# Loading the inputs on one queue in the order of need, keeping TensorE busy until the first projection, and counting table loads in the schedule model

## The chip, the cores and the metric

The kernel runs on one core of a Trainium2 chip. The metric is the time of one execution in microseconds on the device; lower is better. The engines are TensorE (PE: matmuls and their weight loads), ScalarE (ACT), VectorE (DVE), GpSimd (POOL) and SyncE (SP, which issues nearly all transfers here). Each has its own instruction stream and runs it in order; semaphores tie the streams together.

## The reference

Two branches work on the same input x of 2048 tokens by 512 features, in bfloat16, and a gate for each token mixes them.

```python
x = A_x                                            # (1, 2048, 512)
g = sigmoid((x * gate_w).sum(-1, keepdims=True))
return g * A(x, wq, wk, wv, wo, beta) + (1 - g) * B(x, w_gate, w_up, w_down)
# B: (gelu(x @ w_gate) * (x @ w_up)) @ w_down, 1792 hidden features
# A: 32 heads of 16, 4 segments of 512 tokens; for each segment s:
logits = qs @ ks.T * scale + causal_mask;  a_dot = softmax(logits) @ vs
pq = phi(qs)                                       # phi(t) = t+1 if t > 0 else exp(t)
a_mem = (pq @ M) / (pq @ z + 1e-6)
o = sigmoid(beta) * a_mem + (1 - sigmoid(beta)) * a_dot
M = M + phi(ks).T @ vs;  z = z + phi(ks).sum()     # then the next segment; o @ wo at the end
```

So segment s+1 needs the memory M, z of segments up to s, but only its own K, Q and V for the softmax part.

## The kernel before, in words

All weights stay in SBUF. The work goes by segment: `prep(s)` projects K, Q and V from the transposed input `xT` (three buffers), `memory(s)` builds phi(K) and adds to M, z (`mzacc`, `mzbd`), `attention(s)` computes the logits into the four PSUM banks `psXALL` (L703), takes Exp on ScalarE (L711, 20 activations of 128x2048 a segment), masks on GpSimd (L723), multiplies with V into the one bank `psP` (L736), transposes and normalises on VectorE (`norm`, L756 to L764). `ups` and `downs` are the second half of branch B and the output products. All projections, gates, ups and downs share three PSUM banks `psW`; their matmuls all have line L408, their evictions L422 (ScalarE) or L425 (VectorE).

ScalarE must change its function table between Exp and Gelu. So the program has four phases: in phase p all Exp work of segment p (and the preparations of the next segment that need Exp), then a run of Gelu activations (`gelu_phase`: from SBUF at L802, from PSUM at L813), then Exp again. Each change shows as an ACT_TABLE_LOAD.

The order of instructions on every engine is made by a list scheduler, `Sched`, when the program is built. A task has an estimated duration for each engine it may run on, and a priority: the longest chain of estimates behind it plus a bias. At each step the scheduler takes the task with the earliest possible start, then the higher priority. Transfers are modelled with 330 KB per us behind one another. The durations of tasks decide the order alone; on the chip, semaphores decide when each instruction runs. In the model an Exp activation of 128x2048 is `act_t(2048)`, and the first Gelu of a phase has 1.3 added; the first Exp after a Gelu phase, named `exp{s}_0A0`, has nothing added.

At the start of the program:

- `warmP` and `warm0` to `warm7` (L491, L495) are nine matmuls on zeros, with nothing to wait for but a VectorE memset.
- x for segment 0 comes in four transfers of 128 KB into `hT[1]` (named `xin`), issued by SP. TensorE transposes it (`x0t0` to `x0t3`, L500, four 128x128 each against `ident`) into `psW` banks, and ScalarE and VectorE copy it to `xT[0]`.
- wk, wq and the vector gate_w are issued by ScalarE; wv, beta, the first half of w_gate (`wg`), the four transposing transfers of x for segment 1 (`xdma(1)`, L435), the second half of wg, w_up, w_down and wo by SP, in that order. SP's order comes from `rank`, which falls by 20 for each transfer and is its bias; the four small `betaT` transfers have no bias and come after wo.
- Later SP issues further transposing transfers: phi(K) into `phkt` for the memory, x for segments 2 and 3, and `otok` into `oT`; and the 16 output tiles.

The memory part of segment s (`prep` of s > 0) runs during phase s-1: `den` and four `num` products into `psW`, read by VectorE into `ndsc` and `otok` (L637 to L650).

Of the kernel before, what the change touches and what calls it, by code (L numbers as in the profile page):

```python
# [6 lines left out]
PE, ACT, DVE, POOL, SP = "pe", "act", "dve", "pool", "sp"  # L7
# [10 lines left out]
DF = 1792  # L18
NFT = 14
P = 128  # L20
# [293 lines left out]
def mm_t(n):  # L314
    return max(0.026, n / 2370.0)
# [14 lines left out]
def build(nc, A_x, A_wq, A_wk, A_wv, A_wo, A_beta, B_x, B_w_gate, B_w_up, B_w_down, gate_w, out):  # L330
    with ExitStack() as es:
        return _build(es, nc, A_x, A_wq, A_wk, A_wv, A_wo, A_beta, B_w_gate, B_w_up, B_w_down, gate_w, out)


def _build(es, nc, A_x, A_wq, A_wk, A_wv, A_wo, A_beta, B_w_gate, B_w_up, B_w_down, gate_w, out):
    def sb(name, shape, dtype=BF):
        return es.enter_context(nc.sbuf_tensor(name, shape, dtype))
# [15 lines left out]
    hT = [sb(f"hT{i}", [P, NFT, 512]) for i in range(2)]  # L353
# [6 lines left out]
    gatew = sb("gatew", [P, 4])  # L360
# [8 lines left out]
    betaT = sb("betaT", [P, 8])  # L369
# [8 lines left out]
    wq = sb("wq", [P, 4, 512])  # L378
    wk = sb("wk", [P, 4, 512])
    wv = sb("wv", [P, 4, 512])  # L380
    wo = sb("wo", [P, 4, 512])
    wg = sb("wg", [P, 4, DF])
# [5 lines left out]
    Pb = es.enter_context(nc.psum_tensor("psP", [P, 512], F32))  # L388
# [9 lines left out]
    def sem(name):  # L398
        nsem[0] += 1
        return es.enter_context(nc.semaphore(f"{name}_{nsem[0]}"))  # L400

    S = Sched(N_W)

    def task(name, eng, instrs, **kw):
        return S.add(Task(name, {eng: instrs}, **kw))
# [12 lines left out]
    def copy_out(name, g, dst, src, reads, writes, n, engs=(ACT, DVE), **kw):  # L418

        alts = {}  # L420
        if ACT in engs:
            alts[ACT] = [Instr(lambda e: e.activation(dst(), src(), ACTF.Copy), reads=reads, writes=writes,  # L422
                               est=act_t(n))]
        if DVE in engs:
            alts[DVE] = [Instr(lambda e: e.tensor_copy(dst(), src()), reads=reads, writes=writes,  # L425
                               est=dve_t(n))]
        return S.add(Task(name, alts, grp=g, **kw))

    def dma(name, eng, out_ap, in_ap, reads, writes, nbytes, issue=0.7, transpose=False, bias=0.0, sm=None,
            nonc=False):  # L430
        sm = sm if sm is not None else sem("d")

        def f(e):
            if transpose:
                return e.dma_start_transpose(out_ap(), in_ap())  # L435
            if nonc:
                with nc.allow_non_contiguous_dma(reason="small vector"):
                    return e.dma_start(out_ap(), in_ap())
            return e.dma_start(out_ap(), in_ap())
        return task(name, eng, [Instr(f, reads, writes, issue, dma_sem=sm)], bias=bias, nbytes=nbytes)  # L440

    rank = [9000.0]

    def wdma(key, eng, dst, src, nbytes, nonc=False):
        rank[0] -= 20.0
        dma("w_" + str(key), eng, lambda: dst, lambda: src, [], [("w", key)], nbytes, bias=rank[0], nonc=nonc)

    def xdma(s):
        for kb in range(4):
            rank[0] -= 20.0  # L450
            dma(f"x{s}_{kb}", SP, lambda kb=kb: xT[s % NX][:, kb, :],
                lambda kb=kb: A_x[0, s * 512:(s + 1) * 512, kb * 128:(kb + 1) * 128],
                [], [("xT", s % NX, kb)], 131072, issue=1.25, transpose=True, bias=rank[0] if s < 2 else 0.0)

    r4 = lambda w: w.rearrange("(kb p) n -> p kb n", p=P)
    wgr, wur = r4(B_w_gate), r4(B_w_up)
    half = 7 * 128

    warm = PT[R_PT - 1][:, 0, :]
    wkey = ("PT", R_PT - 1)  # L460
# [6 lines left out]
    task("tload", ACT, [Instr(lambda e: e.activation(stmp[:, 0:1], warm[:, 0:1], ACTF.Exp), reads=[wkey],  # L467
                              writes=[("stmp",)], est=1.5)], bias=8000.0)
    xin = hT[1][:, 0:4, :]
    for a in range(4):  # L470
        rank[0] -= 20.0
        dma(f"x0_{a}", SP, lambda a=a: xin[:, a, :], lambda a=a: A_x[0, a * 128:(a + 1) * 128, :], [],
            [("hT", 1, a)], 131072, bias=rank[0])
    wdma("wk", ACT, wk[:], r4(A_wk), 524288)
    wdma("wq", ACT, wq[:], r4(A_wq), 524288)
    wdma("gatew", ACT, gatew[:], gate_w.rearrange("(kb p) -> p kb", p=P), 1024, nonc=True)
    wdma("wv", SP, wv[:], r4(A_wv), 524288)
    wdma("beta", SP, betab[:], A_beta.partition_broadcast(P), 8192)
    for g in range(4):
        bsrc = A_beta.rearrange("(t g j) -> g t j", g=4, j=2)[g]  # L480
        dma(f"betaT{g}", SP, lambda g=g: betaT[32 * g:32 * g + 32, :].rearrange("p (t j) -> p t j", j=2),
            lambda bsrc=bsrc: bsrc.partition_broadcast(32), [], [("betaT", g)], 1024, nonc=True)
    wdma(("wg", 0), SP, wg[:, :, 0:half], wgr[:, :, 0:half], 917504)
    xdma(1)
    wdma(("wg", 1), SP, wg[:, :, half:DF], wgr[:, :, half:DF], 917504)
    wdma(("wu", 0), SP, wu[:, :, 0:half], wur[:, :, 0:half], 917504)
    wdma(("wu", 1), SP, wu[:, :, half:DF], wur[:, :, half:DF], 917504)
    wdma("wd", SP, wd[:], r4(B_w_down), 1835008)
# [1 line left out]

    task("warmP", PE, [Instr(lambda e: e.matmul(Pb[:, :], warm[:, 0:128], warm, start=True, stop=True), [wkey],  # L491
                             [("P",)], 0.43)], bias=5001.0)
    for i in range(8):
        gw = Grp(banks)
        task(f"warm{i}", PE, [Instr(lambda e, gw=gw: e.matmul(gw.f32()[:, :], warm[:, 0:128], warm, start=True,  # L495
                                                              stop=True), [wkey], [gw.key], 0.43)],
             grp=gw, bias=5000.0 - i)
    for kb in range(4):
        g = Grp(banks)
        task(f"x0t{kb}", PE, [Instr(lambda e, g=g, kb=kb, a=a: e.transpose(  # L500
            g.bf()[:, a * 128:(a + 1) * 128], xin[:, a, kb * 128:(kb + 1) * 128], ident[:, :]),
            [("hT", 1, a), ("c", "ident")], [g.key], mm_t(128)) for a in range(4)], grp=g)
        copy_out(f"x0ev{kb}", g, lambda kb=kb: xT[0][:, kb, :], lambda g=g: g.bf()[:, 0:512], [g.key],
                 [("xT", 0, kb)], 512)

    c = [Instr(lambda e: e.memset(maskc[0][:], 0.0), writes=[("c", "mask", 0)], est=0.1)]
    for g in range(4):
# [7 lines left out]
         bias=3000.0)  # L515
# [14 lines left out]
    def exp_task(phase, name, instrs, **kw):  # L530
        after = list(kw.pop("after", ()))
        if phase > 0:
            after.append(gelu_last[phase - 1])
        t = task(name, ACT, instrs, after=after, **kw)
        exp_tasks[phase].append(t)
        return t

    exp_task(0, "gexp", [
        Instr(lambda e: e.activation(gexp[:], betab[:], ACTF.Exp), [("w", "beta")], [("c", "gexp")], 0.25),
        Instr(lambda e: e.activation(gexpT[:], betaT[:], ACTF.Exp), [("betaT", g) for g in range(4)],  # L540
# [18 lines left out]
    def phi_task(nm, s, phase, src, skey, dst, dkey, i):  # L559
        t0, t1 = 2 * i, 2 * i + 2  # L560
        tk = [(skey, t) for t in range(t0, t1)] if not isinstance(skey, tuple) else \
            [skey + (t,) for t in range(t0, t1)]
        dk = [(dkey, t) for t in range(t0, t1)]
        ex = pex[i]
        exp_task(phase, f"{nm}e{s}_{i}", [Instr(lambda e: e.activation(ex[:], src[:, t0:t1, :], ACTF.Exp),
                                               tk, [("pex", i)], act_t(1024, False))])
        task(f"{nm}c{s}_{i}", DVE, [
            Instr(lambda e: e.tensor_scalar(dst[:, t0:t1, :], src[:, t0:t1, :], 0.0, None, ALU.max), tk, dk,
                  dve_t(1024, 4)),
            Instr(lambda e: e.tensor_scalar(ex[:], ex[:], 1.0, None, ALU.min), [("pex", i)], [("pex", i)],  # L570
                  dve_t(1024, 4)),
            Instr(lambda e: e.tensor_tensor(dst[:, t0:t1, :], dst[:, t0:t1, :], ex[:], ALU.add),
                  dk + [("pex", i)], dk, dve_t(1024, 2))])

    def prep(s):
# [17 lines left out]
        for tile in range(4):  # L593
# [11 lines left out]
                                for tile in range(4) for kb in range(4)], 16)  # L605
        s4 = slice(4 * s, 4 * s + 4)
        exp_task(ph, f"gexs{s}", [Instr(lambda e: e.activation(exs[:, s4], gg.f32()[:, 0:4], ACTF.Exp),
                                        [gg.key], [("exs", s)], 0.25)], grp=gg)
        bc = lambda a: a.rearrange("p (a o) -> p a o", o=1).to_broadcast([P, 4, H])
# [364 lines left out]
```

The softmax here doesn't subtract the row's maximum and nothing guards it: scores larger than these inputs give would overflow.

## Time and profile before

| | |
|---|---|
| median of 3 runs | 298.05 us (297.53 to 298.47) |
| profiled execution | 298.3 us |
| span of its profile | 296.6 us |
| mean granted TensorE clock | 0.983 |
| bytes moved by the transfers | 15.30 MB |

Times in the profile are microseconds from the start of the span; the profiled execution's own time has 1.7 us more than the span. PE stands for TensorE matmuls and PEld for its weight loads, which overlap; the busy shares are averages over all stages. The line of 40 slices gives the busy tenths of each fortieth of the span (7.4 us), and PEclk the clock that was granted to TensorE in tenths. "SPq" is the time in which SP issues transfers. The chain is followed back from the last instruction: at each step to what released it, or to the instruction ahead of it on its engine. A landing is counted from the start of a transfer's issue.

### The profile page before, as it was taken

Reading aid. Unit: us, or ns where it says so; the run is one execution under the profiler, and the core shown is the slowest. Engines: PE = TensorE matmul, PEld = TensorE weight load, DVE = VectorE, ACT = ScalarE, POOL = GpSimd, SP = SyncE. Lnnn points to the kernel's source line nnn. Section 1 sums busy time; section 2 is a strip of 40 time slices with the busy share of each in tenths; the row PEclk is TensorE's granted clock in tenths of the full one; section 3 lists DMA queues with packets and bytes.
Section 4 is the critical chain, followed back from the end, with each engine's and each line's share of the span. In section 5 each row is a group of like instructions: output and inputs, shape, how many; then the busy total and the mean of one; then the engine's idle time right before and its main releaser. Section 6 shows DMA issues by size and latency. Waiting matters only on the chain.

```text
span 296.6 us, 5371 instructions
## 1 busy us (share of the span) xinstructions
PE 277.6 (94%) x2185; PEld 115.2 (39%) x2185; DVE 193.1 (65%) x335; ACT 215.6 (73%) x169; POOL 102.5 (35%) x193
## 2 busy tenths in 40 slices
PE   5999999998899999987998999997998999997995
PEld 1443433334443344342443334433443334333442
DVE  0388899678988655796427783869616773559431
ACT  2387898889999877877579697687768677667202
POOL 7026773341004346733003334563202334433200
PEclk9799999999999999996999999999999999999999
DMA  7999920000024201002002100110003000000002
GB/s 217 246 338 352 114 49 2 0 1 2 18 55 88 56 24 43 7 2 53 2 5 48 38 0 0 38 39 0 2 1 73 2 0 20 35 20 0 2 0 71
DMA packets 29769, 15.30 MB, mean 52 GB/s; under 512 B 21296, under 2 KB 29744, under 8 KB 29744
## 3 DMA queue, kind: packets, MB, share of 16 engines
q1 hardware_dynamic: 28160, 13.91, 18.8%
q10 hardware_dynamic: 1584, 1.05, 1.2%
q8 instruction: 17, 0.28, 0.4%
q14 instruction: 8, 0.07, 0.1%
HBM read 8.14 MB, written 2.10 MB: 35 GB/s over the span
## 4 chain that ended last, share of the span: by engine, by line
PE 74%; ACT 11%; DVE 9%; DMA 2%; issue 2%; SPq 0%; POOL 0%; ACTq 0%; DVEq 0%
PE psW L408 59%; PE psXALL L703 8%; PE psP L736 6%; ACT pt L711 5%; ACT hT L802 3%; DMA hT<-in_A_x_dram 2%; PE psXALL L408 1%; ACT L711 1%; DVE vaug L425 1%; DVE hT L834 1%; DVE kpad_0 L582 1%; DVE kT L425 1%; DVE tb L744 1%; DVE obf L760 1%; DVE kpad_1 L590 1%
## 5 line engine op out<-in xcount | busy, mean ns | idle before, releaser
L711 ACT ACTIVATE pt<-psXALL 128x2048 bf16<-128x2048 f32 x80 | 150.1, 1876 | 45.0 <-PE psXALL L703 33.5
L723 POOL TENSOR_SCALAR_AFFINE_SELECT pt<-pt 128x512 bf16<-128x512 bf16 (+1 forms) x112 | 83.5, 747 | 171.7 <-ACT pt L711 165.0
L408 PE MATMUL psW<-xT,wu 128*128 128x512 bf16 x224 | 53.0, 380 | 4.0 <-DVE hT L834 2.1
L408 PE MATMUL psW<-xT,wg 128*128 128x512 bf16 x224 | 53.0, 389 | 0.0
L408 PE MATMUL psW<-wd,hT 128*128 128x512 bf16 x210 | 50.7, 380 | 0.0
L834 DVE TENSOR_TENSOR hT<-psW,hT 128x512 bf16<-128x512 f32 x56 | 37.7, 686 | 8.6 <-PE psW L408 8.0
L744 DVE STREAM_TRANSPOSE tb<-psP 128x512 f32<-128x512 f32 x32 | 22.8, 713 | 22.8 <-PE psP L736 22.7
L408 PEld LDWEIGHTS psW<-xT,wg 128*128 128x128 bf16 x224 | 21.0, 100 | 27.2 <-issue 4.9
L408 PEld LDWEIGHTS psW<-xT,wu 128*128 128x128 bf16 x224 | 19.8, 98 | 28.9 <-DVE hT L834 3.2
L408 PEld LDWEIGHTS psW<-wd,hT 128*128 128x128 bf16 x210 | 18.9, 97 | 23.7 <-issue 3.6
L736 PE MATMUL psP<-pt,vaug 128*17 128x256 bf16 (+3 forms) x512 | 23.6, 305 | 0.0
L813 ACT ACTIVATE hT<-psW 128x512 bf16<-128x512 f32 x28 | 16.5, 597 | 8.1 <-PE psW L408 8.1
L862 DVE TENSOR_SCALAR ost<-psW,omgt 128x512 bf16<-128x512 f32 x12 | 8.7, 743 | 16.7 <-PE psW L408 16.7
L703 PE MATMUL psXALL<-qT,kpad_1 32*128 32x512 bf16 (+3 forms) x256 | 16.1, 305 | 2.6 <-ACT pt L711 2.4
L703 PE MATMUL psXALL<-qT,kpad_0 32*128 32x512 bf16 (+3 forms) x256 | 15.8, 301 | 2.4 <-ACT pt L711 2.4
L408 PE MATMUL psW<-xT,wk 128*128 128x512 bf16 x64 | 17.0, 395 | 0.1
L408 PE MATMUL psW<-xT,wq 128*128 128x512 bf16 x64 | 16.6, 388 | 0.3 <-DVE qT L425 0.3
L650 DVE TENSOR_TENSOR otok<-psW,ndsc 128x512 bf16<-128x512 f32 x12 | 7.6, 683 | 13.2 <-PE psW L408 13.1
L408 PE MATMUL psW<-wo,oT 128*128 128x512 bf16 x60 | 15.8, 380 | 0.0
L408 PE MATMUL psW<-wv,xT 128*128 128x512 bf16 x64 | 15.5, 380 | 0.0
L736 PEld LDWEIGHTS psP<-pt,vaug 128*17 128x17 bf16 x512 | 10.1, 90 | 13.4 <-issue 6.6
L425 DVE CAST hT<-psW 128x512 bf16<-128x512 f32 x20 | 13.2, 676 | 2.6 <-PE psW L408 2.6
(90 smaller groups left out, 252.6 us busy)
## 6 DMA issues: line engine op xcount, KB each, us to landing
out_dram<-ost SPq DMA_DIRECT2D x16, 128.0 KB, 1.7
wg<-in_B_w_gate_dram SPq DMA_DIRECT2D x2, 896.0 KB, 7.7
wu<-in_B_w_up_dram SPq DMA_DIRECT2D x2, 896.0 KB, 8.2
wd<-in_B_w_down_dram SPq DMA_DIRECT2D x1, 1792.0 KB, 14.9
wk<-in_A_wk_dram ACTq DMA_DIRECT2D x1, 512.0 KB, 4.2
hT<-in_A_x_dram SPq DMA_DIRECT2D x4, 128.0 KB, 5.0
wq<-in_A_wq_dram ACTq DMA_DIRECT2D x1, 512.0 KB, 6.1
wv<-in_A_wv_dram SPq DMA_DIRECT2D x1, 512.0 KB, 8.5
```

Of the source, the lines that this page charges most:

```text
L408: return Instr(lambda e: e.matmul(view(), lhsT, rhs, start=first, stop=last), reads=reads, writes=[fkey if fkey is not None else g.key], e ...
L425: alts[DVE] = [Instr(lambda e: e.tensor_copy(dst(), src()), reads=reads, writes=writes, est=dve_t(n))]
L650: Instr(lambda e, gn=gn, qt=qt: e.tensor_tensor(otok[:, qt, :].rearrange("p (h e) -> p h e", e=16), gn.f32()[:, :].rearrange("p (h e) -> p ...
L703: instrs.append(Instr(lambda e, t=t, g=g, j=j, kb=kb, ncol=ncol, c0=c0: e.matmul(X[g][:, c0:c0 + ncol], kpad[j][sl][32 * g:32 * g + 32, t, ...
L711: prev_exp[0] = exp_task(s, f"exp{s}_{t}{name}", [Instr(lambda e: e.activation(PT[slot][:], XALL[:, :].rearrange("p (g c) -> p g c", g=4), ...
L723: minstrs.append(Instr(lambda e, view=view, pat=pat: e.affine_select(out=view, in_=view, compare_op=ALU.is_ge, fill=0.0, base=0, pattern=p ...
L736: instrs.append(Instr(lambda e, q=q, kb=kb, slot=slot, c0=c0, h=h: e.matmul(Pb[32 * q:32 * q + 17, 128 * kb:512], Vaug[sl][:, kb, h, :], P ...
L744: task(f"pvt{s}_{t}_{j}", DVE, [Instr(lambda e: e.transpose(Tb[i2][:, j, :], Pb[:, :]), [("P",)], [("Tb", i2, j)], dve_t(512))])
L802: t = task(f"gelu{s}_{f0}", ACT, [Instr(lambda e, hv=hv: e.activation(hv, hv, ACTF.Gelu_apprx_tanh), hk, hk, act_t(512 * n, False) + (0.0 ...
L813: lambda e, g=g, ft=ft, s=s: e.activation(hT[s % 2][:, ft, :], g.f32()[:, :], ACTF.Gelu_apprx_tanh),
L834: task(f"Um{s}_{ft}", DVE, [Instr(lambda e, g=g, ft=ft: e.tensor_tensor(hT[sl][:, ft, :], g.f32()[:, :], hT[sl][:, ft, :], ALU.mult), [g.k ...
L862: DVE: [Instr(lambda e, view=view, gt=gt, tile=tile: e.tensor_scalar(ostage[tile][:], view(), omgt[:, gt:gt + 1], None, ALU.mult), rd, [(" ...
```

## The change

x for segment 0 comes in two transfers of 256 KB. All input transfers are issued by SP, in the order x, wk, wq, wv, gate_w, beta, betaT, both halves of wg, x for segment 1, then the rest as before; betaT now has a rank. One warm matmul more is issued, and three more matmuls on zeros (`warmE`, into `psP`) can run once `x0t3` is done. In the schedule model the first Exp after each Gelu phase is 1.3 longer; this changes no instruction, only the order that the scheduler makes.

```diff
-    for a in range(4):
+    for a in range(2):
         rank[0] -= 20.0
-        dma(f"x0_{a}", SP, lambda a=a: xin[:, a, :], lambda a=a: A_x[0, a * 128:(a + 1) * 128, :], [],
-            [("hT", 1, a)], 131072, bias=rank[0])
-    wdma("wk", ACT, wk[:], r4(A_wk), 524288)
-    wdma("wq", ACT, wq[:], r4(A_wq), 524288)
-    wdma("gatew", ACT, gatew[:], gate_w.rearrange("(kb p) -> p kb", p=P), 1024, nonc=True)
+        dma(f"x0_{a}", SP, lambda a=a: xin[:, 2 * a:2 * a + 2, :],
+            lambda a=a: A_x[0, a * 256:(a + 1) * 256, :].rearrange("(t p) d -> p t d", p=P), [],
+            [("hT", 1, 2 * a), ("hT", 1, 2 * a + 1)], 262144, bias=rank[0], issue=0.45)
+    wdma("wk", SP, wk[:], r4(A_wk), 524288)
+    wdma("wq", SP, wq[:], r4(A_wq), 524288)
     wdma("wv", SP, wv[:], r4(A_wv), 524288)
+    wdma("gatew", SP, gatew[:], gate_w.rearrange("(kb p) -> p kb", p=P), 1024, nonc=True)
     wdma("beta", SP, betab[:], A_beta.partition_broadcast(P), 8192)
     for g in range(4):
...
+        rank[0] -= 20.0
         dma(f"betaT{g}", SP, ...
-            ... 1024, nonc=True)
+            ... 1024, nonc=True, bias=rank[0])
     wdma(("wg", 0), SP, wg[:, :, 0:half], wgr[:, :, 0:half], 917504)
+    wdma(("wg", 1), SP, wg[:, :, half:DF], wgr[:, :, half:DF], 917504)
     xdma(1)
-    wdma(("wg", 1), SP, wg[:, :, half:DF], wgr[:, :, half:DF], 917504)
...
-    for i in range(8):
+    for i in range(9):
         gw = Grp(banks)
         task(f"warm{i}", PE, ...
...
+    task("warmE", PE, [Instr(lambda e: e.matmul(Pb[:, :], warm[:, 0:128], warm, start=True, stop=True), [wkey],
+                             [("P",)], 0.3) for _ in range(3)], bias=4.0,
+         after=[t for t in S.tasks if t.name == "x0t3"])
...
         t = task(name, ACT, instrs, after=after, **kw)
+        if phase > 0 and name.endswith("_0A0"):
+            t.est[ACT] += 1.3
         exp_tasks[phase].append(t)
```

## The prediction

> **What bounds the kernel now.** I read the page first, for the bound; then the chain that ended last, for the stages it passes; then the timeline and the stretches by clock window for the head, the transfers' landings, and the waits of TensorE at each return to Exp.
>
> The page:
>
> ```profile
> PE 277.6 (94%) x2185; PEld 115.2 (39%) x2185; DVE 193.1 (65%) x335; ACT 215.6 (73%) x169; POOL 102.5 (35%) x193
> ...
> PE   5999999998899999987998999997998999997995
> ...
> PEclk9799999999999999996999999999999999999999
> ...
> PE 74%; ACT 11%; DVE 9%; DMA 2%; issue 2%; SPq 0%; POOL 0%; ACTq 0%; DVEq 0%
> ```
>
> TensorE works 277.6 of 296.6 us, so only 19 us are idle on it, and three quarters of the chain are its own. A head start therefore reaches the end if TensorE stays fed. Two slices show a lower clock: the second (0.7) and the nineteenth (0.6). The head of the chain:
>
> ```profile
> 2.19 6.06 DMA hT<-in_A_x_dram
> ...
> 8.57 0.60 ACT xT L422
> ...
> 9.83 4.62 PE psW L408 x16
> ```
>
> The kernel waits until 8.25 us for the last of the four pieces of x, and only then transposes and projects. The timeline around it:
>
> ```profile
> 1.66 3.62 PE L495 MATMUL psW<-pt 128*128 128x512 bf16 x8
> 4.35 9.43 SPq L435 DMA_TRANSPOSE xT<-in_A_x_dram  x4
> 8.30 0.58 PEld L500 LDWEIGHTS psW<-ident,hT 128*128 128x128 bf16 x9 [0.63 <-DMA hT<-in_A_x_dram]
> 9.62 1.06 PE L408 MATMUL psW<-xT,wk 128*128 128x512 bf16 x2
> 12.56 1.03 PE L408 MATMUL psW<-xT,wk 128*128 128x512 bf16 x4
> ```
>
> Two projection matmuls need 1.06 us at 9.62, four need 1.03 us at 12.56: the first eight run at half rate. The reason is in the stretches cut at the clock changes (columns: busy time and count per engine, granted clock, DMA):
>
> ```profile
> 5.25:8.66 3.41, 0.95 (x11) 0.56 (x10) 0.00 (x0) 0.09 (x1) 1.81 (x4) 1.00 0.98 279
> 8.66:12.07 3.41, 3.34 (x16) 1.53 (x14) 0.85 (x2) 1.10 (x2) 0.00 (x0) 0.50 0.82 288
> 131.54:134.95 3.41, 0.88 (x7) 0.10 (x4) 3.27 (x7) 2.77 (x2) 1.62 (x2) 1.00 0.00 0
> 134.95:141.78 6.83, 6.36 (x41) 2.54 (x42) 3.61 (x6) 4.64 (x4) 1.91 (x3) 0.50 0.28 58
> ```
>
> Twice a stretch of 3.41 us with under 1 us of TensorE work is followed by half clock. Last, TensorE's waits from 153 to 162 us and from 222 to 230 us, where the second and third Gelu phases return to Exp:
>
> ```profile
> PE psXALL L703 <- ACT pt L711: 1.1, 1, 1.1
> ```
>
> ```profile
> PE psXALL L703 <- ACT pt L711: 0.8, 1, 0.8
> ```
>
> **Part 1, arrival of x.** Its four pieces, issued at 0.81, 1.26, 1.72 and 2.19 us, landed 2.7, 4.2, 5.8 and 6.1 us later, the last at 8.25: wk and wq, issued by ScalarE at 0.81 and 1.30, share the transfers with them. All queues moved 122 GB/s in the third microsecond, then 370, 382 and 357. With x (524 KB) alone at the front, 17 + 122 + 370 KB have gone by at 4.0 us, so x lands at about 4.3. wk's 524 KB more are through at about 5.4, wq's at 6.9, wv's at 8.4 (350 GB/s, 0.2 us to land).
>
> TensorE is then held by the warm matmuls. Nine run from 1.26 to about 5.10 at 0.427 us each; the added tenth ends at 5.3 to 5.5, so x is no longer late and the warm matmuls are. Now from the first of the run of transposes (8.30) to the first projection (9.62) it is 1.32 us, the wait for a bank and an eviction included; the three transposes that had run before 8.30 add 3 x 0.064 (0.58 / 9). That gives 5.4 + 1.32 + 0.19 = 6.9 us. The three "warmE" matmuls stand between the last transposes and the projection: 0.22 us each at full rate, 0.43 at half, so 0.65 to 1.3 us on the path. First projection: 7.55 us (6.9 if they fall into the eviction's wait, 8.2 at half rate), against 9.62: **-2.05 us** (-2.7 to -1.4). Its weights are there (5.6 us), and wq (7.1) is there 0.9 us before its first use at 8.4. Splitting x in two transfers instead of four costs nothing: they end before the warm matmuls do.
>
> **Part 2, the clock.** Now eight projection matmuls take 9.62 to about 12.7, 3.1 us; at full rate 8 x 0.216 = 1.73. After the change the stretch 5.25 to 8.66 would hold about 0.2 us of warm matmul, 1.0 of transposes, 0.65 of warmE and 1.1 of projections, some 3 of 3.4 us, where 0.95 was too little. I take full clock: **-1.35 us** (0 if the stretch still counts as too quiet). The Trainium skill ("TensorE: Matmul & The Clock Gate", section on the HAM clock gate) says that the clock drops after at least one idle window of about 3.4 us, and that the window runs freely. By that rule the 0.95 us of work would have kept the clock up, warmE would buy nothing and its 0.65 us would be a pure cost. The rows above speak otherwise, and the sum goes by them.
>
> **Part 3, the queues.** SP's line gets wk, wq and gatew (0.46 + 0.53 + 0.53 us of issue now on ScalarE) and the four betaT (0.43 to 1.6 each, now at 23.3) ahead of wg, and wg's second half ahead of the transposing loads of xT for segment 1; it loses two issues of x (0.8). The first xT issue slips from 4.35 to 0.81 + 0.84 + 0.46 + 0.53 + 0.56 + 0.53 + 0.56 + 4 x 0.43 + 0.44 + 0.58 + 0.5 for gaps = 7.5 us. In front of it are 4 x 524 + 2 x 917 KB, 3.93 MB: at 350 GB/s from 2.05 us that is 13.3. Now the last of the four landed at 16.0, 2.0 us after wg's first half (3.87 + 10.1); an issue of 1.3 to 1.7 us each allows up to 4. So xT lands at 16 to 18, I take 17. It is first used by the Q projections of segment 1, at 23.34 now and 3.4 earlier then, 19.9. Cover: 3 us, where it was 7; **0**, and up to 2 us lost if transposes stall as the second did here (it was being issued from 5.85 to 10.5). Cover for the rest: wv (8.6) is first used at 14.7 now; wg's first half (about 11.5) at 28.7; gatew at 22.9; wu, wd and wo, behind xT, not before 74 us. ScalarE's three issues go from before its first table load (2.41 us); nothing waits there until the eviction at 8.57. betaT comes earlier, so gexp's two activations (0.22 + 0.21 at 33.3) move into ScalarE's empty head: 0, and at most 0.43 gained.
>
> **Part 4, the 1.3 us on the first Exp of phases 1 to 3.** This adds no instruction. It makes the list scheduler place attention 1.3 us later on ScalarE, so TensorE's order can put other matmuls where it now waits. ScalarE's rows give load 153.99 + 1.28, Exp at 155.28, so 1.3 is the right size. At the three returns TensorE waits 0, 1.05 and 0.79 us for that Exp: the bound is -1.84; on the other side 0, as fillers taken forward can be missing later. I take half: **-0.9**. The Trainium skill ("ScalarE: Activation LUTs", section on what a table load costs) gives 2.66 us per switch with a drain. By that figure the schedule model would still be 1.36 us short at each return and the gain smaller; the rows show no such drain.
>
> **Sum.** -2.05 - 1.35 - 0.9 = -4.3 us. The profiled execution took 298.3 us (span 296.6 and 1.7 around it) and gives 294.0; from the median of the three runs, 298.05, it is **293.8 us**. The terms' bounds alone give 291.7 (-2.7, -1.35, -1.84, -0.43) to 298.7 (-1.4, 0, 0, +2).
>
> **Rivals.** *The gap at 132 us goes (0.15).* Between 130 and 136 us TensorE is idle 3.0 us, waiting for VectorE (1.7 for otok) and ScalarE (1.3), and then runs 6.36 us at half clock, losing 3.2: 6.2 us together. The order there is made anew by a scheduler that only compares start times, so a shift of 1.3 us may dissolve it: 287.6 if all of it goes, 289 to 291 if only the clock stays up.
>
> *The lead is eaten behind xT (0.15).* If the transposes stall behind wg, TensorE waits at the Q projections of segment 1 for 2 us or a little more: 293.8 + 2 = 295.8, and with no gain in part 4 either 296.7; 296 to 298.
>
> *A second gap like that at 132 us (0.17), the slower side.* Place: the end of an attention phase, where VectorE runs the five instructions of norm (3.1 us there) while three banks wait for its otok products. After phases 0 and 2 the otok products come first now (four in 2.48 us at 222.45). If the new order puts norm first there too, it costs another 6.2: 293.8 + 6.2 = 300.0. It decides only when the stretch falls under about 1 us of work and the clock halves; the idle 3.0 us alone leaves 296.8.
>
> *The change doesn't do what it says (0.05).* x would land no sooner because its start and not the sharing set it; against it speaks its first piece, there at 3.5 us. Then only the clock and part 4 are left: 295.8.
>
> **How the numbers follow.** My forecast, 292 to 296, has 0.48. Differences under 0.3%, 0.9 us, can't be told from no change, so faster means under 297.15 and slower over 298.95. Faster: 0.48 + 0.15 + 0.10 of the third case + 0.04 = 0.77. Slower: 0.15 of the second gap and 0.01 elsewhere = 0.16; the rest, 0.07, the same. The range runs from 289.0, which takes in most of the vanished gap, to 299.2, which leaves out most of the second gap: about 0.2 outside.
>
> **What would show it.** Right: both x transfers landed by 4.6 us; the transposes directly after the warm matmuls at 5.3 to 5.5; first projection at 7 to 8.2, with four matmuls in 1.03 us at once; the first Exp of attention near 11.8 (15.22 now); the Gelu phase's first activation near 67 (70.58); TensorE's waits for the Exp after table loads under 1 us in all. Wrong: xT landing after 20 us with a TensorE wait at the Q projections; more than one clock drop after 100 us; or a first Gelu that comes 3 us earlier while the end does not.

## The result, and the profile after

The changed kernel takes 301.93 us (median; 300.62 to 302.80), 1.012 times the time before, with an interval of 1.008 to 1.017. That is 3.7 us more than the four executions of the kernel before that were timed with it (median 298.26), where 293.8 was forecast and 299.2 was the upper end. Its profiled execution took 301.33 us, with a span of 299.6. In all comparisons the ratio leaves out executions more than 1.5% above the fastest of their kernel (three of ten in e3, one each in e1, e5 and e7), while the median keeps them.

The page of the kernel after, first the busy times, the slices of TensorE, its clock and the transfers, then the chain's shares:

```profile
PE 277.6 (93%) x2189; PEld 114.6 (38%) x2189; DVE 192.0 (64%) x333; ACT 216.9 (72%) x171; POOL 103.7 (35%) x193
...
PE   7459999999979999997899999999899999999995
...
PEclk9958999999999999999799999999999999999999
DMA  6299970000013421000300200100001200000002
...
PE 77%; DVE 7%; ACT 5%; DMA 3%; POOL 3%; SPq 2%; issue 2%; ACTq 0%; POOLq 0%
```

TensorE is busy in the second and third slices for only 0.4 and 0.5, where it had 0.9 and 0.9, and the low clock has moved into the third and fourth. In the second slice the transfers show 0.2: neither TensorE nor the transfers do much there. The chain that ended last says who is waited for (start, duration, what):

```profile
7.22 10.48 DMA betaT<-in_A_beta_dram
...
18.65 0.62 PE psXALL L710 x4
19.27 4.38 PE psW L408 x10
```

One of the four betaT transfers, 0.5 KB, holds the chain for 10.48 us. The timeline of the head:

```profile
7.08 1.04 PE L408 MATMUL psW<-xT,wk 128*128 128x512 bf16 x4 [0.23 <-DMA wk<-in_A_wk_dram]
...
9.31 13.10 SPq L435 DMA_TRANSPOSE xT<-in_A_x_dram  x4
...
10.33 1.03 PE L408 MATMUL psW<-xT,wq 128*128 128x512 bf16 x4
11.31 0.23 ACT L546 ACTIVATE gexp<-betab 128x32 f32<-128x32 bf16 x1 [2.56 <-DMA betab<-in_A_beta_dram]
17.82 0.21 ACT L547 ACTIVATE gexpT<-betaT 128x8 f32<-128x8 bf16 x1 [6.28 <-DMA betaT<-in_A_beta_dram]
17.93 0.58 ACT L422 ACTIVATE qT<-psW 128x512 bf16<-128x512 f32 x1
18.06 0.17 DVE L550 TENSOR_SCALAR gexpT<-gexpT 128x8 f32<-128x8 f32 x1 [8.66 <-ACT gexpT L547]
...
18.65 0.62 PE L710 MATMUL psXALL<-qT,kpad_0 32*128 32x512 bf16 x4 [7.30 <-DVE gtmp L553]
19.37 1.88 ACT L718 ACTIVATE pt<-psXALL 128x2048 bf16<-128x2048 f32 x1 [0.37 <-PE psXALL L710]
```

Read it from top to bottom. The first projection comes at 7.08 and runs at full rate: four matmuls in 1.04 us at once. It leads by 2.54 us, where 2.05 was forecast. Then ScalarE, which runs its stream in order, stands 2.56 us for beta and 6.28 us for betaT, in front of the two gexp activations. Right behind gexpT stands the eviction of Q (its move from PSUM to SBUF), whose matmuls had ended by 9.63. Until it runs, the three banks psW stay full from the projections that end at 11.36, and the logits have no Q. VectorE stands still too, for its task behind gexpT comes ahead of more evictions in its own stream. So TensorE idles 7.30 us; the profile names VectorE's gtmp as the last release, but the chain shows what that hangs on. The first Exp starts at 19.37 instead of 15.22.

The stretches say what the idle time does to the clock, and what the transfers do meanwhile (columns as before: PE, PEld, DVE, ACT, POOL, granted clock, share of the transfer engines, GB/s):

```profile
11.35:18.65 7.30, 0.01 (x1) 0.03 (x1) 0.53 (x4) 1.02 (x4) 0.00 (x0) 0.69 0.46 166
18.65:24.41 5.76, 5.76 (x23) 1.72 (x24) 3.80 (x10) 3.26 (x4) 0.65 (x1) 0.50 1.36 209
```

```profile
12.00:13.00 1.00, 0.00 (x0) 0.00 (x0) 0.00 (x0) 0.00 (x0) 0.00 (x0) 1.00 0.05 0
...
16.00:17.00 1.00, 0.00 (x0) 0.00 (x0) 0.00 (x0) 0.00 (x0) 0.00 (x0) 0.50 0.97 373
```

After the idle 7.30 us TensorE works 5.76 us at half clock, 2.9 of them lost. From about 9 to 15 us hardly a byte moves (0 to 16 GB/s), although two transfers of 900 KB have been issued, the second by 9.3; they move from 15 us on, with 373 GB/s in the seventeenth. The idle time and the clock together make the head's account at the first Gelu (78.06 against 70.58, +7.48): idle 7.30, clock 2.88 and a wait of 0.48 for wq, less the lead of 2.54 and the 1.35 of the old clock drop, +6.77; 0.7 is not assigned. At the end +3.0 of the span is left; 4.5 is won back on the way, 3.0 of it after the third return to Exp (last stretch, 72.48 before, 69.45 after).

### The profile page after: what moved, and what is told of

Its sections match the earlier page's. It is cut to its first block, busy times and chain, and to the rows that moved or that the text cites. A ratio compares the mean times of both kernels' runs of the same rounds, so it can differ in the third digit from the quotient of the medians.

```text
span 299.6 us, 5379 instructions
## 1 busy us (share of the span) xinstructions
PE 277.6 (93%) x2189; PEld 114.6 (38%) x2189; DVE 192.0 (64%) x333; ACT 216.9 (72%) x171; POOL 103.7 (35%) x193
## 4 chain that ended last, share of the span: by engine, by line
PE 77%; DVE 7%; ACT 5%; DMA 3%; POOL 3%; SPq 2%; issue 2%; ACTq 0%; POOLq 0%
PE psW L408 62%; PE psXALL L710 8%; PE psP L743 6%; ACT pt L718 4%; DMA betaT<-in_A_beta_dram 3%; POOL pt L730 1%; SPq L439 1%; PE psXALL L408 1%; DVE otok L657 1%; POOL exsT L625 1%; DVE kpad_1 L597 1%; SPq L438 1%; DVE ndsc L646 1%; DVE hT L841 1%; DVE tb L751 0%
## 5 line engine op out<-in xcount | busy, mean ns | idle before, releaser
L408 PE MATMUL psW<-xT,wg 128*128 128x512 bf16 x224 | 51.6, 381 | 0.0
L408 PE MATMUL psW<-wd,hT 128*128 128x512 bf16 x210 | 51.6, 380 | 0.0
L408 PE MATMUL psW<-wv,xT 128*128 128x512 bf16 x64 | 17.8, 421 | 0.4 <-DVE vaug L425 0.4
L408 PE MATMUL psW<-xT,wq 128*128 128x512 bf16 x64 | 16.0, 381 | 0.5 <-DMA wq<-in_A_wq_dram 0.5
L425 DVE CAST hT<-psW 128x512 bf16<-128x512 f32 x22 | 14.5, 677 | 2.6 <-PE psW L408 2.5
L408 PE MATMUL psW<-wo,oT 128*128 128x512 bf16 x60 | 15.9, 380 | 0.0
L408 PE MATMUL psW<-xT,wk 128*128 128x512 bf16 x64 | 15.5, 380 | 0.2 <-DMA wk<-in_A_wk_dram 0.2
L625 POOL COPY exsT<-exs 32x4 f32<-32x4 f32 x64 | 14.2, 222 | 3.7
L710 PEld LDWEIGHTS psXALL<-qT,kpad_0 32*128 32x128 bf16 x256 | 4.5, 92 | 25.3 <-ACT pt L718 13.2
```

The costliest lines, as they stand in the source:

```text
L408: return Instr(lambda e: e.matmul(view(), lhsT, rhs, start=first, stop=last), reads=reads, writes=[fkey if fkey is not None else g.key], e ...
L625: cross = task(f"exsT{s}", POOL, [Instr(lambda e, g=g, c=c: e.tensor_copy(exsT[sl][32 * g:32 * g + 32, c:16:4], exs[32 * c:32 * c + 32, s4 ...
L710: instrs.append(Instr(lambda e, t=t, g=g, j=j, kb=kb, ncol=ncol, c0=c0: e.matmul(X[g][:, c0:c0 + ncol], kpad[j][sl][32 * g:32 * g + 32, t, ...
```

## The experiments

My theory after the result: the loss is one wait, gexpT's, and it is there because the schedule model counts each betaT as 1024 bytes at 330 KB/us, 3 ns, so that it sees no wait where the chip needs 7 to 10 us. The rivals: the transfers themselves (betaT holds up what is queued behind it, xT above all); the warmE matmuls or the new clock; the 1.3 us in the model. The medians and ratios:

| kernel | median us | ratio to before (95%) | gexpT waits, us |
|---|---|---|---|
| before | 298.05 | | 0 |
| after | 301.93 | 1.012 (1.008 to 1.017) | 6.28 |
| e1: after, betaT behind wo again | 292.2 | 0.978 (0.975 to 0.981) | 2.61, at 34 us |
| e2: before, betaT ahead of wg | 300.33 | 1.010 (1.007 to 1.014) | 5.77 |
| e3: after, gexp behind a later Exp | 299.59 | 1.000 (0.996 to 1.003) | 0 |
| e8: after, betaT's true price in the model | 292.61 | 0.982 (0.979 to 0.986) | 0 |
| e7: e3, betaT issued by ScalarE | 299.27 | 1.003 (1.001 to 1.005) | 0 |
| e4: before, the 1.3 us alone | 295.49 | 0.992 (0.989 to 0.994) | 0 |
| e6: after, without the 1.3 us | 302.13 | 1.013 (1.011 to 1.016) | 5.60 |
| e9: e1 without the 1.3 us | 294.52 | 0.985 (0.981 to 0.989) | 3.02 |
| e5: e1 without the extra warm matmuls | 293.69 | 0.983 (0.980 to 0.987) | 1.94 |
| e10: e9 without the extra warm matmuls | 294.21 | 0.985 (0.981 to 0.989) | 1.00 |
| e11: e1, xT ahead of wg's second half | 294.13 | 0.986 (0.983 to 0.990) | 4.38 |
| e12: e11, beta behind wo too | 294.41 | 0.988 (0.985 to 0.991) | 2.65 |
| e13: e1 with betaT's true price | 291.79 | 0.977 (0.975 to 0.979) | 0 |
| e14: e11 with betaT's true price | 292.02 | 0.980 (0.977 to 0.983) | 0 |

**Is it betaT's place?** e1 takes it back and leaves all else; e2 does nothing but this to the kernel before.

```diff
# e1, on after
-        rank[0] -= 20.0
         dma(f"betaT{g}", SP, ...
-            ... 1024, nonc=True, bias=rank[0])
+            ... 1024, nonc=True)
# e2, on before: the same lines the other way round
```

> The changed kernel with one part undone: the four betaT transfers have no rank again and are issued after wo. Theory 1 (the head is lost because gexpT, placed early in ScalarE's order, waits for the late betaT while the evictions of the first projections stand behind it): ScalarE no longer waits there, the first Exp of attention comes at 11 to 12.5 us (19.4 in the changed kernel, 15.2 before), no clock drop in the first 30 us, first Gelu at 66 to 69, time 292 to 297. Theory 2 (the new order of the later phases is the loss): the first Exp may be early, but the time stays at 299 to 302. Theory 3 (the transposing loads of x for segment 1, now behind both halves of wg, are the loss): TensorE waits 2 to 5 us at the Q projections of segment 1 near 20 us, time 297 to 300.

> The kernel before with one part of the change alone: the four betaT transfers get a rank and are issued before wg. Theory 1: gexpT goes to the front of ScalarE's order and waits for betaT until 15 to 19 us; the first Exp comes at 17 to 21 us instead of 15.2, TensorE waits 4 to 8 us there and its clock halves; time 302 to 307. Theories 2 and 3: the four small transfers are harmless, time 297 to 299.

e1's timeline:

```profile
7.79 1.03 PE L408 MATMUL psW<-xT,wk 128*128 128x512 bf16 x4
...
9.87 0.60 ACT L422 ACTIVATE qT<-psW 128x512 bf16<-128x512 f32 x1 [0.43 <-PE psW L408]
...
11.16 1.88 ACT L717 ACTIVATE pt<-psXALL 128x2048 bf16<-128x2048 f32 x1 [0.69 <-PE psXALL L709]
```

With betaT at its old place the eviction of Q runs at 9.87 instead of 17.93 and the first Exp at 11.16; the first Gelu comes at 67.02. The kernel is 2.2% faster than before. So this one move, with all that the scheduler makes of it, cost 9.7 us between the medians, and the rest of the change is a gain of 6.

e2's timeline shows the same wait without any other part of the change:

```profile
16.40 0.21 ACT L541 ACTIVATE gexpT<-betaT 128x8 f32<-128x8 bf16 x1 [5.77 <-DMA betaT<-in_A_beta_dram]
16.52 1.07 ACT L422 ACTIVATE kT<-psW 128x512 bf16<-128x512 f32 x2
```

Here TensorE waits 3.58 us for the evictions that follow, and a clock drop follows from 15.9 to 22.7. The profile is of the longest of e2's seven executions (303.17 us, mean clock 0.977). Five of the seven took 300.04 to 300.48 us with a mean clock of 0.994, which leaves room for 3.6 us at half rate in 300, so a drop of 6.8 us did not follow in them. The direction is as expected, the loss of 1.0% is smaller than the 302 to 307 us that I had named: TensorE, whose old head came later, has 3.58 us left to wait where it had 7.30 in the changed kernel.

**The wait, or the transfers behind?** e3 leaves the transfers and lets gexp run only after a later Exp activation of attention, `exp0_0B1`. e8 leaves the transfers' order and tells the model what betaT costs, 2 us each by its own rate. e7 is e3 with betaT issued on ScalarE's queue, where it is not in front of wg.

```diff
# e3, on after (gexp_t is the task "gexp")
+    late = [t for t in S.tasks if t.name == "exp0_0B1"][0]
+    gexp_t.preds.add(late)
+    late.succs.add(gexp_t)
# e8, on after: the size in betaT's dma(...), read by the model alone
-            ... 1024, nonc=True, bias=rank[0])
+            ... 660000, nonc=True, bias=rank[0])
# e7, on e3
-        dma(f"betaT{g}", SP, ...
+        dma(f"betaT{g}", ACT, ...
```

> The changed kernel with all transfers in its order, but the two gexp activations may only be placed after the sixth Exp activation of attention (exp0_0B1). Theory 1 in its narrow form (the wait in ScalarE's in-order stream is the cost): first Exp at 11 to 12.5 us, time 293 to 298, although betaT still lands at 17 to 18 us. Wide form (the small packets of betaT also hold up wg and x for segment 1 in the same queue): x for segment 1 still lands near 23 us and TensorE waits 2 to 4 us for it near 20 us, so that 1 to 3 us of the gain against e1 are lost. Theory 2: 299 to 302.

> The changed kernel with every transfer in its place, but the schedule model is told 660 KB for each betaT transfer instead of 1 KB (2 us each at its 330 KB per us, near the 1.2 to 2 us between their landings in the changed kernel). The model then places gexp after the sixth Exp and the first Gate products of segment 0 ahead of the Q projections of segment 1. If the fault was the model's blindness for small packets, the first Exp comes at 11.2 us and TensorE waits under 2 us for wg's first half near 20 us: 292 to 296. If the queue's delay costs the same whichever product stands first, as in e3: 296 to 300.

> The kernel of e3 (gexp late) with the four betaT transfers issued by ScalarE, at its start, instead of SP. If the delay of wg and of x for segment 1 in e3 is one of order within SP's queue, x for segment 1 lands at 16 to 18 us as in e1, TensorE doesn't wait at the Q projections of segment 1, and the time is 291.3 to 293. If the 4-byte packets take the transfer engines' time itself, x for segment 1 lands at 20 us or later, TensorE waits 1 to 3 us, time 294 to 300.

In e3 gexpT waits for nothing and the first Exp comes at 11.12, but the lead is lost a little later. TensorE's waits up to 32 us begin with:

```profile
PE psW L408 <- DMA xT<-in_A_x_dram: 2.7, 1, 2.7
```

The Q projections of segment 1 stand until 23.24, the clock is halved from 23.04 to 26.46, and the first Gelu comes at 71.05. So there are two prices on betaT's place: the wait on ScalarE, and behind it xT, held up by small transfers. With the wait on ScalarE gone, the kernel is level with before (1.000); the 2.2% that e1 is ahead of it are still lost. The runs of e3 lie from 296.2 to 301.6. The seven that the ratio keeps go from 296.2 at a mean clock of 0.994 to 300.1 at 0.977, and the only profile, of one at 296.89 and 0.988, doesn't show where the longer ones lose their time.

In e8 the model knows. gexp now runs at 23.94, and the first gate projections (21.06) run ahead of the Q projections of segment 1 (25.19):

```profile
24.06 0.21 ACT L547 ACTIVATE gexpT<-betaT 128x8 f32<-128x8 bf16 x1
```

```profile
PE psW L408 <- DMA xT<-in_A_x_dram: 0.7, 1, 0.7
```

Nothing is waited for at gexpT, xT costs 0.7 instead of 2.7, the clock does not drop in the head, and the time is 292.61. SP issues the transfers in the same order as in the changed kernel. So the new order of transfers doesn't cost 9 us by itself; it does so with the order of tasks that was made from a wrong price. I call this shown: four numbers that only the planner reads take the loss away, as the old order of transfers does in e1.

In e7 I had expected the delay to end with SP's queue freed. The time did not improve (1.003, against 1.000 in e3). The only profile of e7 is of the longest of its ten executions (302.86 us, where the median is 299.27), so it shows where the time went in that one alone. In it TensorE does not wait for xT any more. It waits for wq and x instead:

```profile
PE psW L408 <- DMA wq<-in_A_wq_dram: 2.5, 1, 2.5
...
PE psW L502 <- DMA hT<-in_A_x_dram: 1.3, 1, 1.3
```

wq in e7, then in the changed kernel (KB, us from issue to landing):

```profile
wq<-in_A_wq_dram SPq DMA_DIRECT2D x1, 512.0 KB, 10.3
```

```profile
wq<-in_A_wq_dram SPq DMA_DIRECT2D x1, 512.0 KB, 6.2
```

wk took 7.4 instead of 5.2 us and wv 11.3 instead of 7.1. The queue that carried nothing but the four betaT shows 576 packets for its 2 KB. Whether the other nine executions lost their time in the same place is not shown. The Trainium skill ("DMA: Bandwidth & Descriptors", section "Issuing engines are not separate DMA queues") says that transfers issued by different engines run on the same 16 transfer engines and interleave. The later landings of wk, wq and wv in this one profile agree with that.

**The 1.3 us in the model.** Alone on before (e4), and taken out of after (e6) and of e1 (e9).

```diff
# e4, on before; e6 and e9 take the same two lines out
+        if phase > 0 and name.endswith("_0A0"):
+            t.est[ACT] += 1.3
```

> The kernel before with one part of the change alone: 1.3 us added to the first Exp after each Gelu phase in the schedule model. As predicted (part 4): the waits of TensorE for that Exp near 157 and 226 us shrink from 1.05 and 0.79 to under 0.5 each, time 296.3 to 298. Theory 2: the new order brings a longer gap elsewhere, time 299.5 to 303. The head up to 30 us is as before in both.

> The changed kernel without the 1.3 us for the table loads in the schedule model. If that part brings 2 to 3 us whatever the head does (e4 against the kernel before), the waits of TensorE for the first Exp after the second and third Gelu phase come back (about 1 us each) and the time is 303.5 to 305. If the order around a late head matters more, 300 to 303. First Exp at 19 to 20 us in both.

> The kernel of e1 (the changed kernel with betaT after wo) without the 1.3 us for the table loads in the schedule model: the head alone. By the prediction's terms the head brings 3.4 us, from 298.2 to 294.8, and the waits of TensorE for the first Exp after the second and third Gelu phase are there (about 1 us each): 294 to 296. If the table-load term brings nothing once the head has changed, as in e6 against the changed kernel, 291.5 to 293.

e4 gains 2.6 us, nearly three times the term of 0.9. The last stretch, from the third return to the end, in before, e4 and after:

```profile
224.12:296.60 72.48, 67.09 (x500) 26.92 (x497) 39.05 (x61) 39.60 (x23) 20.39 (x28) 1.00 0.09 23
```

```profile
224.27:293.70 69.43, 64.40 (x483) 26.12 (x490) 36.13 (x58) 40.18 (x24) 20.82 (x28) 1.00 0.09 24
```

```profile
230.15:299.60 69.45, 65.30 (x492) 26.17 (x490) 36.13 (x58) 40.18 (x24) 20.82 (x28) 1.00 0.09 24
```

Count the weight loads, since matmul records can be missing: 497 behind the third return before, 490 in both others. In e4 the return itself comes no later (224.27 against 224.12), so seven matmuls, some 1.5 us at 0.216, and three VectorE instructions have moved into idle time ahead of it. The rest is the wait of 0.79 that is gone and a wait near 272 us, 1.58 for VectorE before and 1.15 for ScalarE in e4: 1.5 + 0.8 + 0.4 = 2.7 of the 3.05. This is also where the changed kernel wins its 3.0 back.

e6 is as fast as after. I had put 303.5 to 305 first, and 300 to 303 if the order around a late head mattered more; it was the second. Its profile shows half clock in the head for 6.83 us, against 10.24 in after, and a first Gelu at 76.97 against 78.06, so the head gave back 1.1 us of the 2.0 that the tail lost: from the first Exp after the first Gelu phase to the end it takes 209.6 us against 207.6. Over four pairs that differ in the 1.3 us alone this stretch gets shorter by 3.1 (before to e4), 2.0 (e6 to after), 0.4 (e9 to e1) and 1.5 (e10 to e5). Always a gain in these profiles, never the same; after and e1 have one stretch of 3.41 us at half clock in it that e6 and e9 do not have. In the medians two pairs gain over 2 us (e4 2.6, e1 2.3) and two hardly anything (after 0.2, e5 0.5).

**The warm matmuls and the order alone.**

```diff
# e5, on e1; e10 does it on e9
-    for i in range(9):
+    for i in range(8):
...
-    task("warmE", PE, ...
```

> The kernel of e1 (the changed kernel with betaT after wo) without the tenth warm matmul and without the three warmE matmuls. By the prediction's terms: the first projection comes 0.65 to 0.9 us earlier (7.8 in e1), if its weights are there, which land at about 7.0; and if the stretch of 3.41 us around the transposes is then too quiet, the clock halves at the first projections and costs up to 1.35 us, time 292.0 to 293.0. If the clock stays up without them, time 290.8 to 291.6. If the place of the free-running clock window decides, both times appear.

> The kernel before with the new order of the transfers alone: one queue, x in two transfers, betaT after wo; no table loads in the model, eight warm matmuls, no warmE. By the prediction's terms x is there when the warm matmuls end, so the first projection comes near 7.8 us in any case; if the clock then halves for the first projections, 1.35 us are lost against e9: 295.5 to 297. If the clock stays up without the extra matmuls: within 0.7 us of e9.

e5 cannot be told from e1, nor e10 from e9. In both profiles the clock stays up without the extra matmuls; the stretch after the first clock window in e5, then in e10:

```profile
7.20:10.61 3.41, 2.61 (x12) 1.06 (x13) 0.88 (x3) 0.67 (x2) 0.01 (x1) 1.00 0.75 206
```

```profile
7.04:10.45 3.41, 2.61 (x12) 1.06 (x13) 1.04 (x3) 0.82 (x3) 0.16 (x1) 1.00 0.86 220
```

The early x alone puts 2.61 us of work into that window. The first projection of e10 starts at 7.47, against 7.79 in e1, after a wait of 0.47 for wk, that of e5 at 7.80 after 0.80: without warmE it only waits for wk instead. e5 is a miss all the same. Its median of 293.69 is above both cases that I had named (290.8 to 291.6 and 292.0 to 293.0), and its five kept executions go from 291.25 at a mean clock of 1.000 to 295.25 at 0.988. The queue order alone gives 1.5% (e10), as much as the whole head (e9).

**Can the rest be had?** After e1 a wait of 2.61 us at gexpT is left, near 34 us, behind xT and the big weights. e11 and e12 move transfers; e13 and e14 correct the price.

```diff
# e11, on e1
+    xdma(1)
     wdma(("wg", 1), SP, wg[:, :, half:DF], wgr[:, :, half:DF], 917504)
-    xdma(1)
# e12, on e11: wdma("beta", ...) moved behind wo
# e13, on e1, and e14, on e11: 1024 -> 660000 in betaT's dma(...)
```

> The kernel of e1 (the changed kernel with betaT after wo) with x for segment 1 ahead of the second half of wg again, as in the kernel before. The schedule is otherwise the same instruction by instruction on the compute engines, so only the transfers differ. In e1 the last of the four transposing loads lands near 21 us, just when the Q projections of segment 1 want it. If that short cover costs e1 time in some executions, e11 lands them near 18 us and is at 291.0 to 292.5 with less spread; if not, the same as e1 within 0.3%. If the later second half of wg is then missed by the Gate products, 292.5 to 294.

> The kernel of e11 with the 8 KB transfer of beta (one 64-byte packet for each partition) issued after wo as well. If small packets ahead of wg and x for segment 1 cost time there, the transposing loads land another 0.5 to 1.5 us earlier; the time is 0 to 0.5 us below e11, as TensorE didn't wait for them any more. Nothing else should move: gexp is not placed before the tenth Exp in either.

> The kernel of e1 (the changed kernel with betaT after wo), with the schedule model told 660 KB for each betaT transfer. In e1 gexpT still waits 2.6 us for betaT near 31 us and TensorE 1.0 us behind it. The model now places gexp after the exp0_1B1 activation, near 37 us, when betaT has landed (34 to 35.5). If a wait in ScalarE's stream for betaT is what is left of the loss, that wait is 0, the time is 290.3 to 291.5, 0.3 to 0.6% under e1. If not, the same as e1 or slower (291.5 to 293).

> The kernel of e11 (as e1, with x for segment 1 ahead of the second half of wg) with the same 660 KB in the model. e11 was about 2 us slower than e1 and TensorE waited 2.8 us there behind gexpT's wait of 4.4 us for betaT. If that wait is the whole difference, e14 is within 0.3% of e13, 290.3 to 292. If the place of the second half of wg costs by itself, e14 stays 1 to 2 us above e13.

e11 is slower than e1, and its timeline shows the old mechanism once more:

```profile
35.61 0.21 ACT L546 ACTIVATE gexpT<-betaT 128x8 f32<-128x8 bf16 x1 [4.38 <-DMA betaT<-in_A_beta_dram]
...
35.93 1.04 PE L408 MATMUL psW<-xT,wg 128*128 128x512 bf16 x4 [2.80 <-ACT exs L613]
```

e12's wait is 2.65 us and its time no better, against what I expected. With the price corrected the wait is gone in e13 and e14, and the two orders are within 0.3% of each other: with the right price the place of xT makes no difference that these runs can tell. That e11 lost its time to gexpT's wait is not shown: e12 waits there about as long as e1 (2.65 against 2.61) and is still 1.0% slower than e1. e13, the fastest, cannot be told from e1, though I had expected 0.3 to 0.6%. In its profile the first Gelu comes at 65.89 instead of 67.02, but around 132 us TensorE waits 1.6 us for otok and runs two clock windows at half rate instead of one, and the 1.1 us is given back by the second return to Exp (152.05 against 151.49). This profile is of the longest of five executions (292.71 us, mean clock 0.988); three of the others have 0.994, and where those lose their lead is not shown.

## Why the prediction was wrong, by its own steps

**Part 3 failed, at the term for betaT**: "betaT comes earlier, so gexp's two activations (0.22 + 0.21 at 33.3) move into ScalarE's empty head: 0, and at most 0.43 gained." I costed the instruction that moves and not the wait that moves with it. The profile of before had the rows (duration of an issue in ns, first and last start in us; then us from issue to landing):

```profile
L438 SPq DMA_DIRECT2D betaT<-in_A_beta_dram x4: 431/433/1595, 23.3 to 25.9; - x4
...
DMA to landing us min/median/max: 7.5/7.8/9.2
```

betaT needed 7.5 to 9.2 us to land there, from 23.3 us on, where nobody waited. Issued from 5.8 to 7.7, as in the changed kernel, it could by these rows not be there before 13 to 17, which is 3 to 7 us later than the evictions queued behind gexpT. Nor did I name what is queued there: the evictions of Q and K, three psW banks, and TensorE. That sum would have given +3 to +7 and a clock drop, instead of 0. The runs showed a wait of 6.28 us on ScalarE and 7.30 on TensorE, and the move measured 9.7 us at the end (after against e1). The wait on ScalarE alone is not all of it: e3, which takes only that away, wins 2.3 us in the medians and 1.2% in the ratios. The rest is in part the next term; the one profile of e3 does not show all of it.

**Part 3, the cover of xT.** I took "0, and up to 2 us lost", from bytes ahead in the queue at 350 GB/s, with xT at 17 us. In after the four were still being issued at 22.4, and e3, where gexpT's wait no longer hides them, waited 2.7 us for them and lost clock. A count of bytes gave four small transfers no time at all. The bytes were also too kind to the big ones: wk, wq and wv each landed 1.4 us after the estimate (7.0, 8.5, 10.0), which showed as waits of 0.23 and 0.48.

**Parts 1 and 2 held, with some luck.** Forecast: first projection 7.55 at full rate, first Exp near 11.8, first Gelu near 67. Measured: 7.08 in after, and in e1, where part 3's fault is gone, 7.79, 11.16 and 67.02. The 0.7 between after and e1 does not come from the change: the same nine warm matmuls took 3.23 us in the one profile and 4.05 in the other, where the clock rose later. The head alone was put at -3.4 and gave 1.5%, some 4.5 us (e9, e10). The reason given for the clock was half wrong: warmE was not needed, since the earlier projections fill the window (e5, e10). And the -1.35 came from one profile with a mean clock of 0.983. Of the 16 executions of before that were timed with e1, seven have 0.994, which leaves room for one stretch of 3.41 us at half rate where that profile has three, so the drop in the head need not be there each time.

**Part 4** had the mechanism right, TensorE's order filling the waits at the returns, and the size too small: 0.9 against 2.6 (e4). I bounded it by the waits that the trace put down to the Exp, 1.84 in all. The planner also moved work ahead of the return into idle time that I had not counted. Beside another head the term is not the same: 0.2 to 2.3 us in the medians of the other three pairs.

**The rivals.** The gap at 132 us did not go and did not double: after runs 3.41 us at half clock behind it (from 143.9), where before had 6.83. The case "eaten behind xT" was there, but second in line (e3). The slower side came by a way that stood in no case: an in-order engine made to wait for a landing, for which the profile of before had the rows.

## What to carry to other kernels

When a transfer is moved forward in a list-scheduled program, look for the first instruction that reads it, put the landing time measured in the trace beside its new start, and name what stands behind it in that engine's stream: the reader moves too. Check the model's price of every transfer against its landing, small ones first; where it is wrong, correcting the price (e8) repairs the order without touching a transfer. A gain that a schedule model brings is found by counting what moved across the return and not by the waits there alone.

## What the runs showed of the hardware

Four transfers of 0.5 KB in 4-byte pieces landed 6.7, 7.9, 9.4 and 10.5 us after issue in the changed kernel. From 9 to 15 us, with all four issued, the transfer engines showed a busy share of 0.03 to 0.16 and two transfers of 900 KB issued behind them hardly moved; a busy share says little about whether a queue can be used. In e1, with gatew and beta still ahead of these two but betaT behind them, the bytes flow again from 10 us on:

```profile
9.00:10.00 1.00, 1.00 (x6) 0.49 (x5) 0.52 (x2) 0.57 (x2) 0.00 (x0) 1.00 0.40 73
10.00:11.00 1.00, 1.00 (x9) 0.24 (x7) 0.35 (x2) 0.47 (x1) 0.00 (x0) 1.00 0.69 244
```

With betaT issued on another queue the kernel was no faster (e7, 1.003, against e3, 1.000). Why so few bytes take so long was not tried apart.

The clock fell after windows of 3.41 us with 0.95 and 0.88 us of TensorE work and stayed after windows with 2.61. The 16 traces narrow this, if each is cut into steps of 3.41 us from a change of the clock on. From 3 us on, a step at full clock with up to 1.65 us of TensorE work was always followed by half clock, one with more than 2.19 never. In between both happen, so the busy time of one step does not decide alone. From e1 (half clock followed), e11 (full clock followed) and e2 (half clock followed):

```profile
129.91:133.33 3.42, 1.65 (x10) 0.41 (x8) 3.38 (x7) 2.78 (x2) 1.36 (x2) 1.00 0.00 0
```

```profile
132.73:136.14 3.41, 1.69 (x10) 0.41 (x8) 3.38 (x6) 2.77 (x2) 1.42 (x2) 1.00 0.00 0
```

```profile
138.79:142.20 3.41, 2.19 (x29) 0.94 (x32) 3.25 (x7) 2.68 (x2) 1.12 (x2) 1.00 0.00 0
```

The same program does not meet half clock equally often. By an estimate from these lengths, one step at half rate lowers the mean clock of a span of 297 us by 3.41 / 2 / 297 = 0.006; before's profile has three and 0.983. The 16 executions of before beside e1 show 0.994 seven times, 0.988 three times and 0.983 six times.
